# Loading q and k by eights of heads, with one DMA for each pair of heads, in a kernel of attention and soft mixture of experts

## The chip, the cores and the metric

The kernel runs on one core of a Trainium2 chip. The metric is the device time of one execution in microseconds. "Before" is the kernel as it stood, "after" the changed one. Some executions were slow (over 1.5% above the fastest of the same kernel); the medians quoted include them, the ratios do not. Where a ratio is given, it is the mean time of one kernel's fast runs over the mean of the other's fast runs of the same rounds on the same chip, which is not quite the ratio of the medians quoted beside it.

## The reference, cut to what matters

```python
# q, k, v: (8, 12, 448, 64) f32: 8 batches of 12 heads of 448 tokens
q_n, k_n = rmsnorm(q, g_q), rmsnorm(k, g_k)        # over the 64 numbers of a token
attn = softmax(q_n @ k_n.T / 8)                    # per head
x = (attn @ v) -> (3584, 768)                      # heads side by side
logits = x @ phi                                   # 32 slots, 4 for each of 8 experts
slot_input = softmax(logits, over tokens).T @ x
slot_out[e] = relu(slot_input[e] @ w1[e]) @ w2[e]  # w1: 768x1024, w2: 1024x768, f32
out = softmax(logits, over slots) @ slot_out       # (3584, 768)
```

q, k and v are 33 MB in f32, the sixteen expert matrices 50 MB in f32 (cast to bf16 by the DMA), the output 11 MB.

## The kernel before

The kernel handles four heads at a time, a *unit* Q; 24 units make the attention. The sync engine (SP) issues the DMAs of q, k, v and the output, GpSimd those of the weights. The loads and the loop around them:

```python
def load(Q, t):                       # q or k of one unit: one DMA on all 128 partitions
    src = (q, k)[t][Q // QB, Q % QB * 4:Q % QB * 4 + 4].rearrange("h t d -> (h t) d")
    nc.sync.dma_start(out=raw(Q, t), in_=src.rearrange("(r p s) d -> p r (s d)", r=2, s=NT))

def loadv(Q):                         # v of one unit: four DMAs on 64 partitions each
    for r in range(2):
        src = v[...2 heads...].rearrange("h (p s) d -> p h (s d)", s=NT)
        m = (4 - r) * D
        nc.sync.dma_start(out=vraw(Q)[0:64, :, 4 * D * r:4 * D * r + m], in_=src[:, :, :m])
        nc.sync.dma_start(out=vraw(Q)[64:128, :, 3 * D * r:3 * D * r + NT * D - m], in_=src[:, :, m:])

WQ = [0, 2, 4, 7, 9, 12, 14, 16, 18, 20, 21, 21, 22, NQ, NQ]
for Q in range(NQ + 2):
    load(Q + 4, 1); load(Q + 5, 0)    # k four units ahead, q five
    ...                               # squares, row sums, scaling, transposes of later units
    loadv(Q + 3)                      # waits for a free one of two v buffers
    ...                               # seven score / exponential / value steps of unit Q
    for i, wq in enumerate(WQ):       # one or two weight matrices at fixed units
        if wq == Q:
            loadw(i)
```

(Lines are joined and conditions left out here.) A pair of units therefore takes 12 DMAs of SP: 4 of q and k, 8 of v. The framework that builds the program gives each DMA of SP one of eight semaphores in turn; the trace shows it, in that nearly every DMA of SP counts up the semaphore that the one eight places before it had (153 of 157 in the kernel before, with four small ones of ScalarE counted in), and never more than eight are under way. So a DMA cannot go out before the one eight places earlier has landed.

The softmax here doesn't subtract the row's maximum and nothing guards it: scores larger than these inputs give would overflow.

## Time and profile before

| | before |
|---|---|
| time, median of 4 runs beside the changed kernel | 284.26 us (283.14 to 286.06) |
| first exponential; unit 2; unit 18 starts | 13.3; 31.1; 159.1 us |
| last exponential ends | 208.8 us |
| expert stage | 215.9 to 247.9 us |
| output | 248 us to the end, 34 us |

The prediction below shows the page, the stretches and the chain of the expert stage.

The waits of the sync engine, kernel before (line of the waiting DMA, what it waited for, then microseconds in total, how often, the longest):

```profile
SPq L121 <- POOL arena L209: 51.8, 19, 5.0
SPq L121 <- DMA arena<-in_k_dram: 15.1, 13, 3.1
SPq L122 <- DMA arena<-in_q_dram: 10.8, 7, 2.3
```

SP's largest wait on inputs is for GpSimd to have copied an older v out of its buffer (51.8 us). The rows that name a DMA are waits for a landing.

### The profile page before, as it was taken

To read this page: it belongs to the slowest core of one execution; us is meant where nothing else is said; L and a number is where in the kernel's file an instruction comes from. 1 tells how busy PE (TensorE), PEld (TensorE's weight loads), DVE (VectorE), ACT (ScalarE), POOL (GpSimd) and SP (SyncE) were. 2 spreads that over 40 slices of the span, in tenths; PEclk is the share of its full clock that TensorE was granted. 3 is DMA by queue.
4 is the path that set the end of the run, shared out by engine and by line. 5 is a ranking of instruction groups with operands and counts; after the bars stand their busy time and mean duration, and the time that the engine had idled before them with its cause. 6 is when DMAs were issued, how large, how long until landed. Compare 5 with 4: busy or idle time off the path is not lost.

```text
span 282.3 us, 8543 instructions
## 1 busy us (share of the span) xinstructions
PE 224.2 (79%) x3588; PEld 148.7 (53%) x3588; DVE 175.5 (62%) x381; ACT 191.8 (68%) x270; POOL 169.6 (60%) x189
## 2 busy tenths in 40 slices
PE   7568888998599999999989978988978655788800
PEld 3234554755365576566556545655657645743300
DVE  3756777888268889879878865866563101148800
ACT  4798999899379989998998967878850000036600
POOL 0779999994869998999999966788322000000000
PEclk9859999999789999999999995999996555555555
DMA  6999999999999999999999999969999999528997
GB/s 188 303 256 256 256 265 244 268 254 264 237 246 252 270 262 244 277 235 255 274 254 264 238 261 247 251 145 206 201 208 212 212 211 210 104 94 356 412 412 290
DMA packets 45079, 69.82 MB, mean 247 GB/s; under 512 B 3952, under 2 KB 36720, under 8 KB 45040
## 3 DMA queue, kind: packets, MB, share of 16 engines
q1 hardware_dynamic: 29328, 44.05, 53.2%
q0 software_dynamic: 15392, 25.22, 49.2%
q8 instruction: 28, 0.46, 0.6%
q14 instruction: 11, 0.09, 0.1%
q10 hardware_dynamic: 320, 0.00, 0.1%
HBM read 83.46 MB, written 11.01 MB: 335 GB/s over the span
## 4 chain that ended last, share of the span: by engine, by line
PE 31%; DMA 27%; POOL 16%; ACT 8%; issue 7%; DVE 4%; SPq 0%; POOLq 0%; ACTq 0%
DMA arena<-in_v_dram 19%; POOL arena L199 11%; DMA arena<-in_q_dram 9%; PE ov L253 6%; ACT arena L242 5%; PE sc L241 4%; PE hTp L463 4%; PE op L503 4%; PE soTp L473 4%; PE qkTp L217 3%; PE op L504 2%; POOL arena L207 2%; PE sinp L294 1%; DVE ss L187 1%; PE lg L283 1%
## 5 line engine op out<-in xcount | busy, mean ns | idle before, releaser
L242 ACT ACTIVATE arena<-sc 128x896 bf16<-128x896 f32 x168 | 144.6, 916 | 12.9 <-PE sc L241 10.1
L199 POOL TENSOR_TENSOR arena<-arena,rs 128x896 bf16<-128x896 f32 x48 | 82.2, 1715 | 17.4 <-ACT rs L192 15.9
L253 PE MATMUL ov<-arena 128*128 128x65 bf16 (+1 forms) x1344 | 64.9, 201 | 0.2 <-ACT arena L242 0.2
L253 PEld LDWEIGHTS <-arena 128*128 128x128 bf16 x1344 | 50.6, 99 | 20.0 <-issue 19.7
L241 PE MATMUL sc<-arena 64*128 64x448 bf16 x288 | 54.3, 373 | 7.4 <-ACT arena L242 6.6
L187 DVE TENSOR_REDUCE ss<-arena 128x14 f32<-128x896 f32 x48 | 51.6, 1077 | 8.4 <-ACT arena L179 8.4
L263 DVE TENSOR_TENSOR arena<-ov,rd 128x256 bf16<-128x256 f32 x96 | 40.8, 425 | 3.3
L507 ACT ACTIVATE wown<-op,arena 128x768 f32<-128x768 f32 x14 | 12.4, 900 | 42.5 <-PE op L504 42.5
L217 PE MATMUL qkTp<-ident,arena 128*128 128x128 bf16 x336 | 27.1, 226 | 16.2 <-POOL arena L199 15.5
L177 POOL TENSOR_TENSOR arena<-arena 128x896 f32<-128x896 f32 x21 | 35.4, 1688 | 0.2
L179 ACT ACTIVATE arena<-arena 128x896 f32<-128x896 f32 x27 | 25.6, 951 | 11.3 <-DMA arena<-in_q_dram 9.7
L217 PEld LDWEIGHTS <-arena 128*128 128x128 bf16 x336 | 19.7, 100 | 24.8 <-POOL arena L199 20.1
L241 PEld LDWEIGHTS <-arena 64*128 64x128 bf16 x288 | 16.6, 93 | 25.6 <-issue 13.8
L262 DVE RECIPROCAL rd<-ov 128x4 f32<-128x4 f32 x96 | 17.1, 178 | 12.9 <-PE ov L253 12.4
L224 DVE COPY arena<-qkTp 128x896 bf16<-128x896 bf16 x24 | 14.9, 622 | 11.8 <-PE qkTp L217 11.3
L222 DVE TENSOR_SCALAR arena<-qkTp,gg 128x896 bf16<-128x896 bf16 x24 | 16.4, 684 | 7.0 <-PE qkTp L217 6.7
L274 PE MATMUL xTp<-ident,arena 128*128 128x128 bf16 x192 | 18.1, 227 | 2.2 <-DVE arena L263 1.7
L277 DVE COPY arena<-xTp 128x1024 bf16<-128x1024 bf16 x24 | 16.4, 683 | 5.5 <-PE xTp L274 5.5
L207 POOL CAST arena<-arena 128x384 bf16<-128x384 f32 x24 | 12.3, 514 | 9.4 <-DMA arena<-in_v_dram 8.3
L503 PE MATMUL op<-arena,eT 32*128 32x512 bf16 x28 | 16.0, 616 | 1.4 <-ACT wown L507 0.7
L509 DVE TENSOR_SCALAR wown<-op,arena 128x768 f32<-128x768 f32 x14 | 14.2, 1017 | 4.6 <-PE op L504 4.4
L274 PEld LDWEIGHTS <-arena 128*128 128x128 bf16 x192 | 11.3, 100 | 9.9 <-DVE arena L263 5.9
(61 smaller groups left out, 204.6 us busy)
## 6 DMA issues: line engine op xcount, KB each, us to landing
wown<-in_moe_w_dram POOLq DMA_DIRECT2D x10, 1536.0 KB, 16.4
arena<-in_q_dram SPq DMA_DIRECT2D x24, 448.0 KB, 10.4
arena<-in_k_dram SPq DMA_DIRECT2D x24, 448.0 KB, 9.3
out_dram<-wown SPq DMA_DIRECT2D x11, 768.0 KB, 8.5
arena<-in_moe_w_dram POOLq DMA_DIRECT2D x5, 1536.0 KB, 19.6
arena<-in_v_dram SPq DMA_DIRECT2D x48, 128.0 KB, 8.0
arena<-in_v_dram SPq DMA_DIRECT2D x48, 96.0 KB, 8.4
out_dram<-wown SPq DMA_DIRECT2D x6, 384.0 KB, 7.1
```

Of the source, the lines that this page charges most:

```text
L177: nc.gpsimd.tensor_tensor(sq(t), r, r, op=MUL)
L179: nc.scalar.activation(out=sq(t), in_=r, func=ACTF.Square)
L187: nc.vector.reduce_sum(sss[n][:, t], sq(t).rearrange("p (r d) -> p r d", d=D), axis=AX)
L199: (eng or nc.gpsimd).tensor_tensor(qkn(Q, t).rearrange("p s (r d) -> p s r d", r=2), raw(Q, t).rearrange("p r (s d) -> p s r d", d=D), rs. ...
L207: nc.gpsimd.tensor_copy(vext(Q)[:, :, 5:8, :D], vr[:, :, 4:7])
L217: nc.tensor.transpose(pts[t][:, i], qkn(Q, t)[:, s], ident)
L241: nc.tensor.matmul(sc[:, j, :S], kT(Q)[r, i // 4, c0:c0 + 128], qT(Q)[r, i // 4], start=True, stop=True)
L242: nc.scalar.activation(out=attn(i), in_=sc[:, :, :S], func=ACTF.Exp, scale=0.125)
L253: nc.tensor.matmul(ovs[half][:, c, o0:o0 + m], attn(i)[:, j, c0:c0 + 128], mov, start=(n == 0 and c == 0), stop=(n == 6), skip_group_check ...
L263: nc.vector.tensor_tensor(xq(Q).rearrange("p c (h w d) -> p c h w d", h=2, w=2)[:, 2 * half:2 * half + 2, :, w], o[:, :, :, :D], rd.to_bro ...
L274: nc.tensor.transpose(xps[Q][:, i], xq(Q)[:, i % 4, i // 4 * 128:i // 4 * 128 + 128], ident)
L503: nc.tensor.matmul(op[:, 0], eTtok(j, s), so4[r, :512], start=True, stop=True, tile_position=tp)
```

## The change

The intent: q and k are loaded for eight heads at once with 14 tokens to a partition, so that a contiguous piece is 3584 B in place of 1792 B. Fewer and larger packets, and a larger share of the DMA engines when they alternate with the weights. Each pair of heads becomes a DMA on 32 partitions. v has to follow the new order of tokens, so its four DMAs for a unit become eight. The space freed late is used for weights.

```diff
-    NPRE = 10
+    NPRE = 9
-    place("rawq", 2 * 2 * NT * D, 4)
-    place("rawk", 2 * 2 * NT * D, 3)
+    for i in range(2):
+        place("rawq", 2 * 4 * NT * D, 1)
+        place("rawk", 2 * 4 * NT * D, 1)
 ...
-    def load(Q, t):
-        src = (q, k)[t][Q // QB, Q % QB * 4:Q % QB * 4 + 4].rearrange("h t d -> (h t) d")
-        nc.sync.dma_start(out=raw(Q, t), in_=src.rearrange("(r p s) d -> p r (s d)", r=2, s=NT))
+    def load(O, t):
+        src = (q, k)[t].rearrange("b h t d -> (b h) (t d)")[8 * O:8 * O + 8].rearrange("(h r) (p x) -> h p r x", r=2, p=32)
+        dst = at(("rawq", "rawk")[t], O).bitcast(F32).rearrange("p (r x) -> p r x", r=2)
+        for h in range(4):
+            nc.sync.dma_start(out=dst[32 * h:32 * h + 32], in_=src[h])
 ...
     def loadv(Q):
+        src = v.rearrange("b h t d -> (b h) (t d)")[4 * Q:4 * Q + 4].rearrange("(w r) (p a x) -> r a p w x", r=2, p=32, a=2)
         for r in range(2):
             m = (4 - r) * D
-            nc.sync.dma_start(out=vraw(Q)[0:64, ...], in_=src[:, :, :m])
-            nc.sync.dma_start(out=vraw(Q)[64:128, ...], in_=src[:, :, m:])
+            for a in range(2):
+                nc.sync.dma_start(out=vraw(Q)[32 * a:32 * a + 32, ...], in_=src[r, a, :, :, :m])
+                nc.sync.dma_start(out=vraw(Q)[64 + 32 * a:96 + 32 * a, ...], in_=src[r, a, :, :, m:])
 ...
-    WQ = [0, 2, 4, 7, 9, 12, 14, 16, 18, 20, 21, 21, 22, NQ, NQ]
+    WQ = [0, 2, 4, 7, 9, 11, 13, 15, 17, 18, 20, 21, 22, NQ - 1, NQ]
```

(Cut: the first eight heads, which are loaded in eight small DMAs each for q and k; the views of the transposes; the order of the first units.) A pair of units now takes 24 DMAs of SP, 8 of q and k and 16 of v, where it took 12.

## The prediction

> **What bounds the kernel now.** I read the page first (span, the 40 slices, DMA queues), then the time table of chosen stretches, then the chain of waits from the end of attention on, and last the DMA issues of the sync queue.
>
> ```profile
> span 282.3 us, 8543 instructions
> ...
> DMA  6999999999999999999999999969999999528997
> GB/s 188 303 256 256 256 265 244 268 254 264 237 246 252 270 262 244 277 235 255 274 254 264 238 261 247 251 145 206 201 208 212 212 211 210 104 94 356 412 412 290
> ...
> q1 hardware_dynamic: 29328, 44.05, 53.2%
> q0 software_dynamic: 15392, 25.22, 49.2%
> ```
>
> The DMA engines are at 90% or more in nearly every slice up to slice 34 (7.06 us each, so to about 240 us). q1 is what SP issues (q, k, v and the output), q0 the expert weights, counted as written in bf16; they are read as f32, so 210 GB/s of weights is 420 GB/s of reads. ScalarE is next: in the loop it is 9.0 to 9.9 busy of each 10 us. The starts of the exponentials (first of each unit Q of four heads) lie 7.2 to 8.0 us apart in most units, but 14.1 us apart at Q=7 and 12.8 us at Q=19: there the loop waits for q and v. So the loop (13.3 to 208.8 us) is ScalarE with DMA stalls of some 15 us; after it the kernel waits for weights, as the chain shows:
>
> ```profile
> 215.86 2.70 PE hTp L463 x96
> 218.56 1.28 PE soTp L473 x48
> 219.84 0.24 PE hTp L463 x9
> 220.08 1.71 issue
> 221.79 1.18 PE hTp L463 x39
> 222.97 1.28 PE soTp L473 x48
> 224.25 1.09 PE hTp L463 x41
> 225.34 2.37 issue
> ```
>
> Five such gaps (1.71, 2.37, 2.37, 2.54, 1.66, sum 10.65 us) stand in the expert stage, 215.9 to 247.9 us. Each falls where a matmul needs the next weight matrix while the DMA engines are full. Without them it is 32.06 - 10.65 = 21.4 us of PE. From 248.3 to the end, 34 us, is output, which the change leaves alone.
>
> How fast each kind of transfer goes is in the stretches where one kind runs alone or with the weights (first column the stretch, last column GB/s written):
>
> ```profile
> 8.00:10.00 2.00, 1.46 (x12) 0.62 (x11) 0.54 (x2) 1.36 (x3) 2.00 (x2) 1.00 1.05 397
> 15.50:16.50 1.00, 1.00 (x6) 0.18 (x4) 0.59 (x1) 1.00 (x2) 0.88 (x3) 0.50 1.12 205
> 13.50:14.50 1.00, 0.36 (x4) 0.10 (x1) 1.00 (x2) 1.00 (x2) 0.13 (x2) 0.50 1.09 224
> 30.00:35.00 5.00, 4.00 (x63) 2.58 (x59) 3.35 (x8) 4.71 (x6) 4.87 (x5) 1.00 1.10 258
> 191.00:197.00 6.00, 4.61 (x71) 3.00 (x68) 3.87 (x9) 4.75 (x8) 5.73 (x8) 1.00 1.16 209
> ```
>
> By the sizes in the trace's packet records, 8 to 10 us is q and k alone (128 partitions a DMA, 397 GB/s); 15.5 to 16.5 is nearly all v (64 partitions a DMA, 205); 13.5 to 14.5 is q and k just after v (224, so they recover slowly); 30 to 35 is q/k beside weights; 191 to 197 weights alone. A 1792 B packet of q takes 74 ns at its best, the v packets (896 B on average) also about 74 ns when v runs alone, though 42 to 50 ns at their best. So a DMA on half the partitions goes at half the rate with all engines "busy".
>
> **What the Trainium skill says.** (1) "SBUF — State Buffer", section "Door 1: The DMA port swizzle": bandwidth depends on how many of 16 ports the partitions reach; 0 to 31 reach 8 ports, as do 0 to 63, and each port is worth about 27 GB/s. The trace agrees for 64 partitions: 205 GB/s, against 218 for eight ports. No run yet shows 32. (2) "DMA: Bandwidth & Descriptors", "Queues, rings and completion order": an engine takes its queues in turn, packet by packet. The packet records agree: at 30 to 35 us q/k at 120 GB/s is 67 packets/us and weights at 139 GB/s is 68, one for one. (3) Same page, "Why small descriptors are slow (HBM only)": a fixed cost per packet. Here it is small: output packets of 3072 and 6144 B took 122 and 238 ns, so about 6 ns are fixed.
>
> **The change part by part.**
>
> *Packets.* q and k go from 1792 B to 3584 B pieces, 12288 packets to 6656 (the first eight heads stay at 1792). Against weights in the other queue that is a larger share: a pair cost 16 x 1792 B / 120 GB/s = 239 ns on an engine; now I estimate 172 ns for a weight packet and 140 to 190 ns for 3584 B, about 345 ns a pair, that is 166 GB/s for q/k and 95 for weights. In reads this is 166 + 190 = 356 GB/s instead of 120 + 278 = 398. The saved fixed cost, 5632 x 6 ns / 16 = 2 us of engine time, is nothing.
>
> *Half the ports.* All q/k DMAs now write 32 partitions, two DMAs into the lower half, then two into the upper. Alone they should go like v, at about 200 GB/s instead of 230 to 400. v stays at half the ports, in twice as many DMAs.
>
> *DMA work to the last v.* Before: 33 MB of q, k, v and nine weights (9 x 3.15 = 28 MB read), 61 MB by 190 us, 325 GB/s. After: nine weights paired half with q/k (345 ns), half with v (205 ns) keep q0 busy some 140 us at about 357 GB/s, which is 50 MB; the remaining 11 MB alone at 200 GB/s take 55 us: 195 us, plus the 2 us before the first packet, and a margin for gaps to 207. So the DMA work up to there ends 7 to 17 us later. Seven weights at 7.5 us (1.573 MB / 0.209) then follow in both kernels if DMA stays the bound.
>
> *Sync queue.* v DMAs go from 96 to 192, q/k from 48 to 104. The rows of the issues:
>
> ```profile
> L121 SPq DMA_DIRECT2D arena<-in_v_dram x48: 595/604/1043, 6.5 to 186.7; - x48
> L110 SPq DMA_DIRECT2D arena<-in_q_dram x24: 367/419/595, 0.7 to 165.0; - x24
> ```
>
> A v issue is 0.60 us whatever its size, 0.67 from one to the next; a q/k one about 0.45, 0.52 with its gap. Two units need 16 x 0.67 + 8 x 0.52 = 14.9 us of SP, against 14.6 us of two ScalarE-bound units (7.3 each) and about 7.5 us before. In all 192 x 0.67 + 104 x 0.52 = 183 us, so SP becomes nearly a bound itself. Also each DMA waits for the one eight places earlier (in the built programs; in the trace the fifth load, with ScalarE's four small ones before it, goes out at 4.10 us as the first lands). Eight v DMAs now hold 0.46 MB, eight before 0.92.
>
> *Start.* The square of unit 2 stands before the first exponential and needs the 4 DMAs of q for eight heads, the 25th to 28th of SP: 16 x 0.52 + 8 x 0.67 + 4 x 0.52 = 15.8 us of issue, landed at about 17.5 us instead of 11.5. First exponential about 18 instead of 13.3. q of the next eights waits behind v2 and v3 (16 x 0.67 us), so Q=2 starts near 44 us rather than 31.1.
>
> *Weights.* Nine own places instead of ten; the tenth weight goes at Q=18 into raw buffers no longer needed, then one per unit at Q=20, 21, 22, 23, 24. q and k end at about Q=18, so q0 has the engines nearly to itself for six units, 44 us, room for five to six weights. Only two or so are left when the experts start: the 10.65 us of gaps mostly vanish, whatever the loop does.
>
> *Engines.* ScalarE squares 26 against 27, VectorE takes two of GpSimd's 48 scalings, a few small logs and exponentials more: under 2 us. The evacuation writes runs of 32 instead of 64 elements; I take 622 and 684 ns to stay.
>
> *Sum.* Q=18 at 44 + 16 x 8.2 = 175 (before 159), six units of 7.4: attention ends near 220 to 225 (208.8), 7 us of joining, 22 us of experts, 34 us of output: 283 to 288 of span; the DMA account, +7 to +17 on everything, gives 290 to 300. Between them: 289.
>
> **Rivals.** *The share wins:* stalls of the loop come from q/k and v starved by weights, and 3584 B packets end that; with engines out of step, 32-partition DMAs need not collide on ports (v beside weights ran at 50 to 59 ns a packet, not 74). Then the loop nears 24 x 7.4 = 178 us, the experts 22: 265 to 272. Against it: the worst stall, 70 to 83 us, has no weight in flight, and q1 alone would now be slower. *SP or the eight in flight become the bound:* any wait of SP for a buffer then adds itself to the loop, 8.5 to 9 us a unit over Q=2 to 18: 295 to 305. For it: SP had waits of 51.8 us for GpSimd's copies of v, which its larger load no longer hides. *A wash:* a loop 10 us longer and gaps 10 us shorter: 283. For it: the same bytes pass the same 16 engines.
>
> **Range and chances.** The centre 289 is just at the +2% line (289.1). The port effect is in the trace, the shorter expert stage almost sure; unsure is how much of the slowness lies beside weights that fill the engines anyway. 273 to 303 should hold it 8 times in 10; faster 0.20, same 0.33, slower 0.47.
>
> **What would show it.** Right: q/k alone near 200 GB/s in the first 20 us; first exponential near 18 us; Q=2 near 44 us; SP issuing almost without pause; expert stage 21 to 24 us without long gaps; attention ending after 215 us. Wrong: q/k alone above 300 GB/s on 32 partitions, SP issues much below 0.5 us, or units at an even 7.3 us; then the time goes to 270. Expert gaps still there would mean that the DMA account holds to the end, and over 295 us.

## More of the kernel before

A ratio times 283 to 286 us, the fast mean of the kernel before, gives microseconds.

The chain that ended last, from the page of the kernel before, by engine:

```profile
PE 31%; DMA 27%; POOL 16%; ACT 8%; issue 7%; DVE 4%; SPq 0%; POOLq 0%; ACTq 0%
```

TensorE and DMA share the end, and GpSimd has a part of it.

## The result, and the profile after

| | before | after |
|---|---|---|
| time, median of 4 runs each | 284.26 us | 324.58 us (322.72 to 326.75) |
| ratio of the fast runs | | 1.1414 (95%: 1.1315 to 1.1513) |
| first exponential; unit 2; unit 18 | 13.3; 31.1; 159.1 us | 19.7; 44.4; 200.7 us |
| mean from unit 2 to unit 18, for one unit | 8.0 us | 9.8 us |
| last exponential ends | 208.8 us | 254.7 us |
| expert stage | 215.9 to 247.9 us | 261.7 to 292.0 us |
| 3584 B or 1792 B packet of q and k, median | 87 ns (1792) | 227 ns (3584) |

The result is correct and slower by 14%. The loop is the whole of it: the last exponential ends 45.9 us later, and after it the kernel after is even a few microseconds shorter. Of the 45.9 us, 13.3 are there when unit 2 starts and 28.3 more come between units 2 and 18.

The page of the kernel after (span; DMA share and GB/s in 40 slices of 8.1 us; the queue of SP's loads; the chain that ended last):

```profile
span 325.0 us, 8750 instructions
...
DMA  6899998999888998979989799899489999905998
GB/s 171 193 203 224 216 227 161 226 254 209 213 184 171 240 243 177 251 162 241 239 185 249 155 246 234 181 246 231 118 158 209 211 211 212 186 4 207 411 409 330
...
q1 hardware_dynamic: 26128, 44.06, 49.4%
...
DMA 49%; PE 19%; SPq 11%; ACT 7%; issue 5%; POOL 3%; DVE 2%; ACTq 0%; POOLq 0%
```

In the slices of the loop the DMA engines are at 8 or 9 tenths nearly throughout, as before, yet move mostly 160 to 250 GB/s where before it was mostly 235 to 300: a busy engine is not a fast one. The chain is now half DMA (49% against 27%), and PE has gone from 31% to 19%. The new entry is SPq, 11% where it was 0%: the end of the program is led back through the issuing queue itself.

Chosen stretches of the kernel after (stretch, then busy time of PE, PEld, DVE, ACT and POOL, the granted clock, the DMA share and GB/s written):

```profile
15.00:21.00 6.00, 1.72 (x11) 0.89 (x11) 3.31 (x4) 3.35 (x7) 4.08 (x5) 0.50 1.05 220
...
54.00:57.00 3.00, 3.00 (x29) 1.83 (x28) 1.57 (x3) 2.85 (x5) 0.55 (x1) 0.50 0.37 100
...
230.00:240.00 10.00, 9.45 (x130) 5.74 (x127) 6.72 (x15) 8.39 (x13) 6.29 (x11) 0.90 0.50 102
```

By packet size, 15 to 21 us is q and k: 220 GB/s at a full DMA share, near what the prediction took for half of the ports. 54 to 57 us is v, with next to nothing beside it: 100 GB/s, and the engines are busy for only 0.37 of the time. They are not full; they are not *given* enough. And at 230 to 240 us, where I had expected the weights to have the engines to themselves, half of the DMA time is idle: the weights are issued by the loop's units, and those are late.

The DMA issues of the kernel after (KB each, median us from issue to landing):

```profile
arena<-in_q_dram SPq DMA_DIRECT2D x44, 224.0 KB, 5.1
...
arena<-in_v_dram SPq DMA_DIRECT2D x96, 64.0 KB, 5.0
```

Before, it was 448 KB in 10.4 us for q and 128 KB in 8.0 us for v. Landing has become quicker, but not in proportion: half of the bytes of v, but 5.0 against 8.0 us. With eight under way of 56 KB on average (the other half of the v DMAs has 48 KB), 8 x 57,344 B / 5.0 us = 92 GB/s: the 100 GB/s of the window. This is the arithmetic of such a stretch.

The sync engine's waits in the kernel after (L125 issues q and k, L145 and L146 v):

```profile
SPq L145 <- DMA arena<-in_k_dram: 28.0, 21, 2.4
SPq L146 <- DMA arena<-in_k_dram: 21.0, 21, 2.3
SPq L125 <- DMA arena<-in_v_dram: 18.1, 26, 1.6
```

The wait for GpSimd's copies of v (51.8 us) has shrunk to some 2 us, in rows of at most 1.0 us, and landings have grown to 98 us (these three rows and four more of 5 to 10 us). The queue was ahead; now it is behind. One issue costs less than the prediction took:

```profile
L145 SPq DMA_DIRECT2D arena<-in_v_dram x96: 311/372/999, 8.7 to 234.2; - x96
```

A v issue on 32 partitions is 0.37 us (minimum, median and maximum are given in ns), not 0.60. All q, k and v issues together still take 121 us (84 before), without the short gaps between them.

The expert stage of the kernel after, the pieces in the chain that answer to the gaps of before:

```profile
265.92 1.60 issue
...
271.07 2.37 issue
...
276.99 2.37 issue
...
282.84 2.46 issue
```

They are 1.60, 2.37, 2.37 and 2.46 us, 8.8 us where there were 10.65. The gaps that were to vanish are there, and the records show that none of them, before or after, is a wait for weights. They cut a matmul group in two that reads one matrix throughout, as here in the kernel before:

```profile
224.11 1.23 PE L463 MATMUL hTp<-arena,wown 128*128 128x4 bf16 x41
227.71 0.33 PE L463 MATMUL hTp<-arena,wown 128*128 128x4 bf16 x7 [2.37 <-issue]
```

Each of the last seven matrices had landed before its first matmul, by 1.5 to 37 us before and 5.7 to 52 us after. The gaps stand 256 TensorE instructions apart (128 weight loads and 128 matmuls), at the same places of the program in both kernels. During each one a single packet of 16,384 B is under way in the queue that carries instructions:

```profile
q8 instruction: 28, 0.46, 0.6%
```

(that is the whole queue, from the page of the kernel before), and the matmuls go on 1.2 to 1.5 us after the packet has ended. So they look like waits for TensorE's own instructions; no run tests that.

### The profile page after: what moved, and what is told of

It is laid out like the page before. It is cut to its first block, busy times and chain, and to the rows that moved or that the text cites. A ratio compares the mean times of both kernels' runs of the same rounds, so it can differ in the third digit from the quotient of the medians.

```text
span 325.0 us, 8750 instructions
## 1 busy us (share of the span) xinstructions
PE 240.5 (74%) x3588; PEld 158.7 (49%) x3588; DVE 181.4 (56%) x383; ACT 193.4 (60%) x277; POOL 168.0 (52%) x188
## 3 DMA queue, kind: packets, MB, share of 16 engines
q1 hardware_dynamic: 26128, 44.06, 49.4%
## 4 chain that ended last, share of the span: by engine, by line
DMA 49%; PE 19%; SPq 11%; ACT 7%; issue 5%; POOL 3%; DVE 2%; ACTq 0%; POOLq 0%
DMA arena<-in_v_dram 26%; DMA arena<-in_q_dram 13%; DMA arena<-in_k_dram 11%; ACT arena L272 5%; SPq L125 5%; PE hTp L521 3%; PE op L561 3%; PE soTp L531 3%; POOL arena L223 3%; PE ov L283 2%; SPq L146 2%; SPq L145 2%; PE op L562 2%; SPq L133 2%; PE sc L271 2%
## 5 line engine op out<-in xcount | busy, mean ns | idle before, releaser
L272 ACT ACTIVATE arena<-sc 128x896 bf16<-128x896 f32 x168 | 145.3, 916 | 22.3 <-PE sc L271 16.9
L223 POOL TENSOR_TENSOR arena<-arena,rs 128x896 bf16<-128x896 f32 x46 | 78.8, 1714 | 33.4 <-ACT rs L216 23.4
L271 PE MATMUL sc<-arena 64*128 64x448 bf16 x288 | 59.5, 408 | 20.0 <-ACT arena L272 19.3
L283 PE MATMUL ov<-arena 128*128 128x65 bf16 (+1 forms) x1344 | 72.0, 211 | 0.2 <-ACT arena L272 0.2
L283 PEld LDWEIGHTS <-arena 128*128 128x128 bf16 x1344 | 56.8, 106 | 23.5 <-issue 23.1
L211 DVE TENSOR_REDUCE ss<-arena 128x14 f32<-128x896 f32 x48 | 51.8, 1079 | 28.8 <-ACT arena L203 15.7
L201 POOL TENSOR_TENSOR arena<-arena 128x896 f32<-128x896 f32 x22 | 37.9, 1722 | 23.7 <-DMA arena<-in_k_dram 10.9
L240 PE MATMUL qkTp<-ident,arena 128*128 128x128 bf16 x336 | 30.6, 245 | 23.7 <-POOL arena L223 23.6
L240 PEld LDWEIGHTS <-arena 128*128 128x128 bf16 x336 | 22.5, 109 | 33.1 <-POOL arena L223 27.5
L271 PEld LDWEIGHTS <-arena 64*128 64x128 bf16 x288 | 16.4, 95 | 41.8 <-issue 31.1
L267 PE MATMUL sc<-arena 64*64 64x448 bf16 x96 | 16.1, 416 | 9.0 <-ACT arena L272 9.0
L215 ACT ACTIVATE ss<-ss,eps 128x28 f32<-128x28 f32 (+1 forms) x30 | 9.4, 312 | 19.2 <-DVE ss L211 19.2
L230 POOL CAST arena<-arena 128x384 bf16<-128x384 f32 x24 | 12.1, 503 | 10.9 <-PE ov L283 5.2
L231 POOL CAST arena<-arena 128x384 bf16<-128x384 f32 x24 | 12.3, 511 | 10.5 <-DMA arena<-in_v_dram 10.5
L304 PE MATMUL xTp<-ident,arena 128*128 128x128 bf16 x192 | 17.1, 235 | 0.3 <-DVE arena L293 0.3
## 6 DMA issues: line engine op xcount, KB each, us to landing
wown<-in_moe_w_dram POOLq DMA_DIRECT2D x9, 1536.0 KB, 15.8
```

Of the source, the lines that this page charges most:

```text
L201: nc.gpsimd.tensor_tensor(s, r, r, op=MUL)
L211: nc.vector.reduce_sum(sss[n][:, t], sq(t).rearrange("p (r d) -> p r d", d=D), axis=AX)
L223: (eng or nc.gpsimd).tensor_tensor(qkn(Q, t).rearrange("p s (r d) -> p s r d", r=2), raw(Q, t).rearrange("p r (s d) -> p s r d", d=D), rs. ...
L240: nc.tensor.transpose(pts[t][:, i], qkn(Q, t)[:, s], ident)
L271: nc.tensor.matmul(sc[:, j, :S], kT(Q)[r, i // 4, c0:c0 + 128], qT(Q)[r, i // 4], start=True, stop=True)
L272: nc.scalar.activation(out=attn(i), in_=sc[:, :, :S], func=ACTF.Exp, scale=0.125)
```

## The experiments

Theories. **Number:** the loss comes from twice the DMAs, because only eight can be under way and SP waits in order; smaller DMAs mean fewer bytes under way. **Ports:** it comes from 32 partitions reaching half of the ports. **Queue time:** it comes from the time that SP takes to issue. **Start:** it comes from the first units being late. Each kernel ran three rounds beside the kernel before. "Wrong on purpose" means that tokens land in the wrong places: the engines' instructions and sizes stay, the numbers are wrong. The diffs are shortened.

### Pairs of heads on every fourth partition (e1_qk_all_ports)

```diff
-            nc.sync.dma_start(out=dst[32 * h:32 * h + 32], in_=src[h])
+            nc.sync.dma_start(out=dst[h::4], in_=src[h])
```

(and the transposes' views to match; a correct result)

> The changed kernel with one difference: pair h of heads goes to every fourth partition (h, h+4, ...) instead of a block of 32, so each DMA of q and k has the same bytes, packets and count, but reaches all 16 ports. Ports as main cause: q/k alone in the first 20 us above 300 GB/s (210 to 240 in the changed kernel), a 3584 B packet at 140 to 160 ns instead of 230, and 20 to 30 of the 40 us come back: 295 to 305 us. Number of DMAs (eight in flight) as main cause: the packets are as much faster, but the time stays at 313 us or more, because SP still waits for a landing eight places earlier. Result stays correct; VectorE reads PSUM with a stride of four elements, which may make the 24+24 evacuations slower.

Measured: 541.12 us. The run says nothing of the time: as far as the waits tell, the framework takes a write to every fourth partition for a write to all that lies between in the buffer, and puts waits where no data is shared. One number of it can be used: a 3584 B packet took 140 ns in the median (227 in the kernel after, though with busier engines; e5 below gives 142). So half of the ports does cost 3584 B packets more than a third of their rate.

### q and k of the kernel before on every fourth partition (e4_before_qk_strided)

```diff
+        for b in range(4):
-        nc.sync.dma_start(out=raw(Q, t), in_=src)
+            nc.sync.dma_start(out=raw(Q, t)[b::4], in_=src[b::4])
```

> The kernel before with one difference: each q or k load is four DMAs on every fourth partition; as many DMAs and packets as in the run on blocks, but all 16 ports. Ports as main cause: q/k alone near 350 to 400 GB/s, time 284 to 292. Number of DMAs as main cause: within 5 us of the run on blocks, 300 or more.

Measured: 549.04 us, a failed experiment for the same reason. The waits of all engines in this run show it:

```profile
PE sc L243 <- DMA arena<-in_q_dram: 194.7, 18, 14.7
```

Score matmuls, which read k and q transposed, wait 194.7 us for the arrival of other raw q. The 1792 B packets took 74 ns in the median.

### q and k of the kernel before in four blocks of 32 partitions (e3_before_qk_blocks)

```diff
+        for b in range(4):
-        nc.sync.dma_start(out=raw(Q, t), in_=src)
+            nc.sync.dma_start(out=raw(Q, t)[32 * b:32 * b + 32], in_=src[32 * b:32 * b + 32])
```

> The kernel before with one difference: each q or k load is four DMAs on blocks of 32 partitions; the packets stay at 1792 B, layout and units as before. Both theories expect it slower; with the run on strided partitions beside it, it splits the loss. Ports: q/k alone falls from 397 to about 200 to 230 GB/s in the first 20 us and the time is 300 to 315. Number alone: as the strided run.

Measured: 321.29 us, ratio 1.1341 (1.1223 to 1.146); the loop ends at 248.5 us. The kernel before with only its q and k DMAs cut in four loses nearly all that the change loses, with neither the larger units nor the later start (first exponential at 14.7 us). It has both 24 DMAs for a pair of units and half of the ports, so the two are still to be told apart. (The time is above the 300 to 315 us expected of the ports; the strided run that was to decide had failed.)

### The same in four DMAs on all 128 partitions (e7_before_qk_four_full)

```diff
+        for r in range(2):
+            for c in (slice(0, 224), slice(224, 448)):
-        nc.sync.dma_start(out=raw(Q, t), in_=src)
+                nc.sync.dma_start(out=raw(Q, t)[:, r, c], in_=src[:, r, c])
```

> The kernel before with each q or k load as four DMAs on all 128 partitions (two head pairs times half of the seven tokens, packets of 896 B). As many DMAs as the run on blocks of 32 (321.3 us), but all ports. Ports as main cause of that run's 37 us: 284 to 295. Number as main cause: 308 to 325. The smaller packets cost at most 12288 x 9 ns / 16 = 7 us of engine time.

Measured: 327.6 us, ratio 1.1453 (1.1389 to 1.1518), even above the 308 to 325 expected of the number. All ports (896 B packets of 41 ns in the median), and as slow as the kernel after. The ports are not needed for a loss of this size. The packets are also half as large here; the next run keeps ports and packets as they were.

### v of the kernel before in eight (e8_before_v_eight)

```diff
-            nc.sync.dma_start(out=vraw(Q)[0:64, ...], in_=src[:, :, :m])
+            for a in (0, 32):
+                nc.sync.dma_start(out=vraw(Q)[a:a + 32, ...], in_=src[a:a + 32, :, :m])
```

(likewise the upper half: 20 DMAs for a pair of units)

> The kernel before with v in eight DMAs of 32 partitions per unit instead of four of 64: same ports (half of them in both), same packets, 20 DMAs a pair of units instead of 12. Number as a cause of its own: 293 to 303. If ports alone matter: within 2% of the kernel before.

Measured: 306.83 us, ratio 1.0721 (1.0657 to 1.0786), some 20 us, more than expected. v was on eight ports in both forms, and its packets were no slower (48 and 59 ns against 54 and 66, mean). What changed is SP's waits:

```profile
SPq L123 <- DMA arena<-in_q_dram: 33.2, 16, 4.6
SPq L122 <- DMA arena<-in_k_dram: 25.7, 11, 4.6
```

These and six smaller rows are 92 us of landings, where before had 46; the waits for GpSimd are nearly gone, as in the kernel after. Nor were the DMA engines fuller: from unit 2 to unit 18 their share is 0.95, against 1.10 before (it can pass 1, since the times of packets that overlap are added).

### The kernel after with v in four (e2_v_in_four)

```diff
-            for a in range(2):
-                nc.sync.dma_start(out=vraw(Q)[32 * a:32 * a + 32, ...], in_=src[r, a, :, :, :m])
-                nc.sync.dma_start(out=vraw(Q)[64 + 32 * a:96 + 32 * a, ...], in_=src[r, a, :, :, m:])
+            nc.sync.dma_start(out=vraw(Q)[0:64, ...], in_=src[r, :, :, :m])
+            nc.sync.dma_start(out=vraw(Q)[64:128, ...], in_=src[r, :, :, m:])
```

(and the transposes' views to match: 16 DMAs for a pair of units, a correct result)

> The changed kernel with one difference: v again in four DMAs of 64 partitions per unit, as before (the evacuation writes keys and queries in natural order for that), so a pair of units has 16 DMAs instead of 24; q and k still on 32 partitions. Number of DMAs as main cause: 15 to 25 us come back, 300 to 310 us, and SP's waits on landings, 98 us in the changed kernel, fall by a third or more. Ports as main cause: 318 to 325 us. Evacuations may take longer, since they write every second element.

Measured: 307.68 us, ratio 1.0897 (1.0802 to 1.0993). Undoing the v half of the change gives back some 15 of the 40 us by the ratios, as expected of the number. The waits for landings fall only from 98 to 86 us and not by the third that was expected; those for GpSimd begin to return:

```profile
SPq L125 <- DMA arena<-in_k_dram: 21.7, 24, 2.4
...
SPq L144 <- POOL arena L232: 14.4, 5, 6.2
```

### The kernel after with q and k on all partitions (e5_qk_128_wrong)

```diff
-        for h in range(4):
-            nc.sync.dma_start(out=dst[32 * h:32 * h + 32], in_=src[h])
+        for r in range(2):
+            nc.sync.dma_start(out=dst[:, r], in_=src[:, r])
```

(wrong; the first two units in one DMA each as before; 20 DMAs for a pair of units)

> The changed kernel, but q and k of eight heads in two DMAs of all 128 partitions (heads 0 to 3, then 4 to 7), packets still 3584 B, and the first two units in one DMA each. The heads then land in an order the rest does not expect, so the result is WRONG ON PURPOSE; all shapes, sizes and engines' work stay. It gives back the ports, and takes 24 DMAs a pair of units to 20, without the false waits that the strided run had. Ports as main cause of q/k: q/k alone above 300 GB/s and 295 to 305 us, what remains being v in eight DMAs (17 us by the run with v in four). Number as main cause: 315 or more, since 20 of 24 DMAs remain.

Measured: 301.72 us, ratio 1.0536 (1.0457 to 1.0615). The packets take 142 ns. This undoes ports and number of q and k together, and some 25 us come back by the ratios; it does not separate them. Its time lies in the range expected of the ports; f1 below, with 24 DMAs on all ports, shows why that is no proof.

### The same with v in four (e6_qk_128_wrong_v_four)

> The run before this one with v also in four DMAs of 64 partitions: 12 DMAs a pair of units on the same ports as the kernel before, but packets of 3584 B, units of eight heads and the new order of the weights. WRONG ON PURPOSE in the same way. If ports and the number of DMAs are the whole loss, it is back at the kernel before or under it: 272 to 288 us. If something else in the change costs time (the longer lookahead at the start, the order of weights, slower evacuations), 292 or more, and the first exponential or the weights' issue times show where.

```diff
-        for h in range(4):
+        for r in range(2):
+            nc.sync.dma_start(out=dst[:, r], in_=src[:, r])             # q and k, as in e5
-            for a in range(2):
+            nc.sync.dma_start(out=vraw(Q)[0:64, ...], in_=src[r, :, :, :m])   # v, as in e2
```

(and the transposes' views, as in e2) That is 12 DMAs for a pair of units, as before, with everything else of the change kept: units of eight heads, 3584 B packets, the later start, nine weight places. Measured: 289.32 us, ratio 1.0126 (1.0066 to 1.0186), between the two expectations. SP is ahead again:

```profile
SPq L141 <- POOL arena L229: 47.1, 20, 6.3
SPq L125 <- POOL arena L219: 36.2, 13, 4.9
SPq L141 <- DMA arena<-in_q_dram: 12.8, 8, 2.9
```

Unit 2 starts at 43.4 us (12.3 later than before), yet the loop ends only 7.0 us later (215.8) and the expert stage is 2.0 us shorter (30.0; it has one gap of TensorE less). From unit 2 to unit 23 a unit takes 7.93 us in the mean (8.19 before). So the rest of the change nearly pays for its own late start, and the start cannot be the main loss.

### The kernel after in number, on all ports (f1_qk_four_full_wrong)

```diff
-        for h in range(4):
-            nc.sync.dma_start(out=dst[32 * h:32 * h + 32], in_=src[h])
+        for r in range(2):
+            for c in (slice(0, 448), slice(448, 896)):
+                nc.sync.dma_start(out=dst[:, r, c], in_=src[:, r, c])
```

> The kernel after with q and k of a unit of two groups in 4 DMAs of all 128 partitions (packets of 1792 B) in place of 4 DMAs of 32 partitions (3584 B); v in eight as before; so 24 DMAs for a pair of units, as after, but with all ports. It fills the tiles with tokens in another order and gives a wrong result on purpose; the instructions of the engines are the same. Theory A (the number of DMAs, with at most eight under way and the issuing queue waiting in order for the landing eight places earlier): as slow as after or nearly, 315 to 326 us, landings on the issuing queue near 90 us or more. Theory B (half the ports of 32 partitions make the loss): 308 us or less.

Measured: 319.86 us, ratio 1.1278 (1.1126 to 1.143). The landings come to 87 us. The packets run at full speed (74 ns for 1792 B in the median), and of the 40 us only some 4 come back by the ratios, less than the width of the interval. At 24 DMAs for a pair the ports matter little (the packets are also half as large as in the kernel after, and the DMA share from unit 2 to unit 18 is 0.91).

### Half of the ports at 12 DMAs (f2_qk_64_wrong_v_four)

```diff
-        for r in range(2):
-            nc.sync.dma_start(out=dst[:, r], in_=src[:, r])
+        for h in (0, 64):
+            nc.sync.dma_start(out=dst[h:h + 64], in_=src[h:h + 64])
```

(an edit of e6)

> The run e6_qk_128_wrong_v_four with q and k on 64 partitions in place of 128: the number of DMAs is the same (12 for a pair of units), the packets are 3584 B in both, but only half of the ports serve them. Wrong result on purpose. Theory A (number): within 2% of e6 (289.3 us), 286 to 295. Theory B (ports): 300 us or more, with the packets of q and k at 230 ns and more in place of about 142.

Measured: 298.87 us, ratio 1.0585 (1.0476 to 1.0693): between the two expectations, so both missed. The packets take 239 ns (153 in e6). Half of the ports is worth 4.6% by the ratios, some 13 us, where the number leaves room. It is a real cost, the second one.

### v of the kernel before in two (g1_before_v_two)

```diff
-        for r in range(2): ...                 # four DMAs of two heads each
+        nc.sync.dma_start(out=dst[0:64, :, D:], in_=src[:, :, :4 * D])        # four heads
+        nc.sync.dma_start(out=dst[64:128, :, :4 * D], in_=src[:, :, 3 * D:])
```

(8 DMAs for a pair of units; 14% more bytes of v)

> The kernel before with v in 2 DMAs for a unit in place of 4 (each of 64 partitions by 4 heads by 256 numbers; some 14% more bytes of v, as the second block of tokens overlaps the first): 8 DMAs for a pair of units in place of 12. A correct result. Theory A (number): faster than before, 280 us or less, if the number of DMAs still costs at 12; if 12 is already free of it, 283 to 289 (the added bytes). Theory B says nothing of it but the added bytes: 285 to 289.

Measured: 296.71 us, ratio 1.0512 (1.0378 to 1.0645): slower, which nobody had expected. SP's waits:

```profile
SPq L120 <- POOL arena L208: 91.8, 22, 5.3
```

A buffer that is filled by one large DMA is free only when all of GpSimd's copies out of that half are done, and the whole queue stands behind it: 91.8 us where there were 51.8. That is what the profile shows; how much of the loss is this and how much the added bytes is not separated. Fewer DMAs pay only as long as landings, and not buffers, are what the queue waits for.

### Four tiny DMAs more for a unit (g2_before_tiny)

```diff
             nc.sync.dma_start(out=vraw(Q)[0:64, ...], in_=src[:, :, :m])
+            nc.sync.dma_start(out=scr[:, i:i + 1], in_=v[0, 0, 0:16, i % D:i % D + 1])   # 16 x 4 B
             nc.sync.dma_start(out=vraw(Q)[64:128, ...], in_=src[:, :, m:])
+            # and once more
```

> The kernel before with four tiny DMAs (16 packets of 4 B) added to each unit beside the four of v: 20 DMAs for a pair of units in place of 12, and next to no bytes more. If a place among the eight under way is what is scarce (theory A in its strict form): 298 to 308 us, as with v in eight. If the splitting of the data itself costs, and not the number of places, 284 to 290 us.

Measured: 313.63 us, ratio 1.1085 (1.0973 to 1.1197), more than expected. 6 KB in all, moved in 96 DMAs, cost 31 us by the ratio. The waits of SP turn to landings as they did when real data was split:

```profile
SPq L117 <- DMA arena<-in_q_dram: 20.8, 10, 4.2
SPq L130 <- DMA arena<-in_k_dram: 17.8, 7, 4.6
```

So it is not the splitting of data. But a tiny DMA takes a place for 4.9 us (median from issue to landing) *and* 0.59 us of SP to issue.

### The queue's time without a place (h1_before_sp_busy, h2_before_sp_busier)

```diff
+    idle_sem = ctx.enter_context(nc.semaphore())
+    def tiny():
+        for _ in range(16):                    # 48 in h2
+            nc.sync.sem_inc(idle_sem)          # nobody waits for it
```

(called where g2 had its four tiny DMAs)

> The kernel before with 64 instructions more for a unit on the issuing queue that only add one to a semaphore nobody waits for, where the run g2_before_tiny had its four tiny DMAs: it takes the queue's time and no place in flight, and moves nothing. How long they take has to be read from the trace ([...]a tiny DMA's issue was 0.6 us, 2.4 us a unit). If the places in flight make the loss: 283 to 290 us. If it was the issuing queue's own time: 300 us or more, like g2.

> As h1_before_sp_busy with 192 such instructions for a unit, three times as much of the queue's time. At some amount the queue itself must become the bound: if 192 take more than the queue's waits of before leave free (an estimate: about 4 us a unit, from 51.8 us of waits for GpSimd and some 46 us for landings over 24 units), the time goes up; if they take under 2.4 us a unit, it stays under 290 us in the theory of the places, and is near g2 in that of the queue's time.

In h1 the added instructions are, by the view of their line:

```profile
L119 SPq EVENT_SEMAPHORE  x1536: 17/17/17, 6.7 to 204.8; - x192
```

Each is 17 ns, but one starts 58.5 ns after the other, so 64 of them are 3.7 us of SP for a unit, more than the 2.4 us that g2's issues added. Measured: h1 296.49 us, ratio 1.0479 (1.0389 to 1.0568), again between the expectations; h2 457.85 us, ratio 1.6181, where 11.2 us are added for a unit and a unit takes 15.6 from unit 2 to unit 18. In h1 SP hardly waits for landings or buffers any more (15 and 17 us); the largest row is:

```profile
SPq L127 <- DMA arena<-in_k_dram: 8.9, 8, 2.1
```

So the queue's time is a cost too, and the expectation that had it free is wrong: 3.7 us is nearly all of the slack of 51.8 and 46 us (4.1 us a unit), and I take it that the slack is not spread evenly over the units. But g2 took a third less of the queue's time and lost 31 us to h1's 14 (0.1085 and 0.0479 of 283). Less of it, in the same places of the program, should not cost more than in h1, so I put at least 17 of g2's 31 us down to the places (with the DMA engines' own work on the 96 tiny transfers, which I estimate at about 3 us from 3,072 packets and semaphore writes of 15 ns on 16 engines).

### A third buffer for v (h3_before_v_three)

```diff
-    place("vraw", 2 * 2 * NT * D, 2)
+    place("vraw", 2 * 2 * NT * D, 3)
```

> The kernel before with three buffers for v as loaded in place of two: the number of DMAs and their sizes stay. The issuing queue's 51.8 us of waits for GpSimd's copies of v should mostly go. If these waits cost the kernel before anything, it gets faster: 275 to 281 us. If they are only slack behind engines that are full (the eight places and the bytes set the time), the waits turn into waits for landings and the time stays 282 to 287.

Measured: 282.82 us (279.8 to 284.12), ratio 0.9967 (0.9838 to 1.0096): no difference that the runs show. SP's waits, again:

```profile
SPq L122 <- DMA arena<-in_q_dram: 22.4, 15, 3.3
SPq L121 <- DMA arena<-in_k_dram: 19.0, 12, 3.5
```

The 51.8 us of waits for v's buffers went, and landings took their place, 78 us in all, at the same time. So waits for landings alone do not make a kernel slow. This kernel, with a correct result, could have beaten both; it does not do so beyond the spread.

### The runs in one table

"Under way" is the mean number of q, k and v DMAs between issue and landing from unit 2 to unit 17, worked out from the records of issue and landing; "landing" is their mean time from issue to landing in the same stretch. The next three columns divide SP's time up to its last load: issuing, waiting for landings (ScalarE's small DMAs included), waiting for buffers (us; an issue's record can begin within a wait, so they overlap by up to 12 us).

| run | DMAs for two units | q, k on half of the ports | under way | landing, us | issuing | landings | buffers | time, us |
| --- | --- | --- | --- | --- | --- | --- | --- | --- |
| g1 | 8 | no | 6.2 | 13.4 | 65 | 23 | 119 | 296.7 |
| before | 12 | no | 6.7 | 9.2 | 84 | 47 | 63 | 284.3 |
| h3 | 12 | no | 7.6 | 10.5 | 84 | 79 | 17 | 282.8 |
| e6 | 12 | no | 6.1 | 8.4 | 80 | 27 | 88 | 289.3 |
| f2 | 12 | yes | 7.2 | 10.8 | 90 | 60 | 60 | 298.9 |
| e2 | 16 | yes | 7.7 | 8.9 | 101 | 86 | 32 | 307.7 |
| e5 | 20 | no | 7.3 | 6.6 | 101 | 96 | 8 | 301.7 |
| e8 | 20 | no | 7.1 | 6.4 | 105 | 93 | 8 | 306.8 |
| g2 | 20, of which 8 tiny | no | 6.7 | 6.2 | 141 | 66 | 13 | 313.6 |
| f1 | 24 | no | 7.0 | 5.9 | 124 | 87 | 7 | 319.9 |
| after | 24 | yes | 7.3 | 6.2 | 121 | 98 | 5 | 324.6 |
| e3 | 24 | yes | 6.7 | 5.4 | 145 | 63 | 12 | 321.3 |
| e7 | 24 | no | 6.4 | 5.1 | 152 | 62 | 14 | 327.6 |

In every row from f2 down, 6.4 to 7.7 are under way on average, and the mean landing does not fall below 5 us. So the four rows with 24 all sent 1.20 to 1.24 DMAs a microsecond, and what a microsecond brings is that many times the size of one. (Kernel before: 0.75 a microsecond, with larger ones.)

The three columns of SP show what the number buys. From e6 to f1 issuing grows by 45 us and landings by 60, and the 88 us of waits for buffers, which were slack, are used up. In e7 and g2, against the kernel before, it is issuing that grows most (68 and 58 us; landings 15 and 19), and on average the eight places are not full. So the number of DMAs costs in both ways, and issuing is no small part of it.

## Why the prediction was wrong

The direction was the likelier one of the prediction (slower 0.47); the time, 324.58 us, lies outside its range of 273 to 303. The step that failed is the loop's pace, 8.2 us a unit: the account of the DMA work behind it assumed that the engines always have work. The runs showed 9.8 us a unit, because SP could not issue and land 24 DMAs for two units any faster, in order and with eight places. Step by step:

**Half the ports: right in mechanism, second in size.** q and k alone went at 220 GB/s where the prediction took about 200, and the packets of 3584 B at 227 ns. f2 against e6 gives it 13 us at 12 DMAs for a pair; after against f1 only 4 us at 24, within the spread.

**Start: right.** "First exponential about 18 instead of 13.3", "Q=2 start near 44 us": 19.7 and 44.4. It is partly luck: the issue of the 28th DMA ended at 14.3 us and not 15.8, and the last of q landed at 18.8 and not 17.5, two errors of opposite sign. But e6, which starts unit 2 at 43.4, ends its loop only 7.0 us late: a late start is partly caught up when SP is ahead.

**Sync queue: wrong in its size, and what decided stood beside it.** "A v issue is 0.60 us whatever its size" failed: 0.37 for half the partitions, 121 us of issue in place of 183 (which include gaps of 0.07 us). The sentence that carried the result had no cost beside it: "Also each DMA waits for the one eight places earlier [...] Eight v DMAs now hold 0.46 MB, eight before 0.92." I had the mechanism and the bytes, and did not divide by the time to landing. It stood only as a rival, "SP or the eight in flight become the bound", priced at 8.5 to 9 us a unit and 295 to 305 us. Measured: 9.8 us a unit. The slack of SP was read right there ("its larger load no longer hides"), its size not: by 63 us of waits for buffers and 47 for landings before, 5 and 98 after, with 37 us more of issuing, SP ran out of it.

**The DMA account, "the work up to there ends 7 to 17 us later": wrong.** It counted bytes by rates and assumed that the engines are always given work. They were not: v alone at 100 GB/s with a DMA share of 0.37, and half of the DMA time idle at 230 to 240 us. By e8, with ports and packets unchanged, eight DMAs more for a pair of units cost 20 us. From e6 (12) to f1 (24), in the kernel after's own form with q and k on all ports, the ratio goes from 1.0126 to 1.1278, which is 33 us of 284 (packets of q and k are 3584 B in e6 and 1792 B in f1). From unit 2 to unit 18 the DMA share fell from 1.10 to 0.98. The account's sum was off too: nine weights are 3,840 packets of 2048 B and 4,096 of 1536 B in the records, so while they last all queues together move 46 MB and not 50, and by its own rates the account ends near 212 us, not 195.

**Sum: "Q=18 at 44 + 16 x 8.2 = 175" failed** on the 8.2, which was the kernel before's pace carried over: 200.7, that is 9.8 a unit.

**Weights: "the 10.65 us of gaps mostly vanish, whatever the loop does": wrong in its reading.** "Each falls where a matmul needs the next weight matrix" does not hold in the trace it was read from: the matrix had landed every time, and the gaps stand 256 instructions apart in both kernels (see above). 8.8 us of them stayed, and 10.65 us could never be won by earlier weights. The room of 44 us was not used either: the issue times of the late weights follow the units, from the tenth on at 212.8, 235.6, 239.2, 245.4, 253.8 us, just as late as the loop.

**Engines and output: right.** The exponentials take 145.3 us (144.6 before), GpSimd's whole work 168.0 (169.6).

**Packets: right but worth little.** q1 fell from 29,328 to 26,128 packets, by 3,200 and not 5,632, as the added DMAs brought 2,432 packets of 4 B; no run shows a gain from it.

So the change's loss, in the ratios of the runs: the rest of the change (start, eights, nine places) 3.6 us (e6), the number of DMAs 33 us (e6 to f1), the half ports 4 us at that number (f1 to after). That the number costs of itself is shown by e8 and g2. That it acts through the eight places as well as through SP's time for issuing is argued from g2 and h1 (at least 17 of 31 us to the places there; the rest may be the queue's own time). How the 33 us divide between these two in the changed kernel itself is not shown: no run could give more than eight places, since the framework fixes them.

The rule that would have helped is in the Trainium skill, "SBUF — State Buffer", section "The DMA setup-cost knee": every DMA pays about 2 us that do not scale with its bytes, so that 64 KiB at a time reaches about 30% of the best rate. The trace agrees in direction, though with eight under way: v in DMAs of 48 and 64 KB ran at 100 GB/s. I looked up the ports on that page and not this section.

## What to carry to other kernels

Before cutting a DMA into several, count how many of them may be under way at once, and divide: places times bytes of one, by the time from issue to landing, is the most that the queue can bring, and an engine that is 90% busy on average does not show it. Add up what the issues themselves cost beside it. Read the waits of the issuing queue first: here waits for buffers were slack, and none of the kernels that lost more than 30 us had over 15 us of them left (the failed e1 and e4 aside). Before counting on a gap to vanish, check that what it seems to wait for had not landed already. And a transfer that is issued by the loop's progress does not come early when the loop is slow.

## What the Trainium skill lacked or had wrong

- No page that I found has the limit of this framework, eight semaphores in turn for the DMAs of the issuing queues, nor what it costs. Never more than eight were under way in the records before and after; 96 DMAs of 64 B each cost 31 us by the ratio (g2).
- "SBUF — State Buffer", section "The DMA setup-cost knee", advises 32 partitions rather than 64 where 128 can't be had ("same bandwidth, half the SBUF"). No run here contradicts that, but as a way of splitting the same bytes it cost 20 us, since it doubled the number of DMAs: v in eight DMAs of 32 partitions took 306.83 us, in four of 64 286.41 us in the same rounds (e8).
- "DMA: Bandwidth & Descriptors", section "Rules for kernel authors", says to coalesce into one large transfer without a counterweight. With two DMAs of v for a unit in place of four the kernel was slower, 296.71 us, with 91.8 us of waits for a buffer that one large DMA frees only as a whole (g1; part of it may be the 14% more bytes).
- No page that I found warns that writes to every fourth partition can bring waits between data that have nothing in common (it seems that the framework takes them for writes to all the bytes between): 541 and 549 us (e1, e4).
- No page that I found has the pace of plain semaphore increments on the sync engine: one in 58.5 ns, though the record of each shows 17 ns (h1, h2).
